# A ninth block of the spectral product moves behind the scans, and sixteen scans move ahead of the attention steps

## The chip, the cores and the metric

The kernel runs on one core of a Trainium2 chip. Its time is the device time of one execution in microseconds (us). The engines are PE (matrix products, with its weight loads listed as PEld), DVE (vector), ACT (activations), POOL (general) and SP, which here only issues DMAs.

## What is computed

Two branches over the same x (2048 x 512) are mixed by a gate; all in float32.

```python
def _A_ref(x, wqkv, wo):
    H = 32; Dh = D // H            # Dh = 16
    q, k, v = ...                  # x @ wqkv, split into heads
    scores = jnp.einsum("bhqd,bhkd->bhqk", q, k) * Dh ** -0.5
    p = _softmax(scores, axis=-1)
    o = jnp.einsum("bhqk,bhkd->bhqd", p, v)
    return o... @ wo

def _B_ref(x, dft_seq_re, dft_seq_im, dft_hid_re, dft_hid_im):
    a = jnp.einsum("bsd,ed->bse", x, dft_hid_re)
    b = jnp.einsum("bsd,ed->bse", x, dft_hid_im)
    return jnp.einsum("ts,bse->bte", dft_seq_re, a) - jnp.einsum("ts,bse->bte", dft_seq_im, b)

g = _sigmoid((x * gate_w).sum(-1, keepdims=True))
return g * _A_ref(x, A_wqkv, A_wo) + (1 - g) * _B_ref(x, ...)
```

## The kernel before

The 32 heads are handled as 16 pairs. For each pair the kernel needs two passes over the scores: a **scan**, which finds the largest score of each query, and a **use**, which computes the scores again, shifted by that maximum, takes the exponential and multiplies with the values. One scan (number n, from 0 to 1023, 64 for each pair) is one block of 128 queries against 512 keys for both heads of the pair: two matmuls and their maxima. Scans run in the order of n all through the kernel.

The order of the work is written out by hand; each engine's queue holds its instructions in the order of the program. It has three stages.

**Projections** (up to about 288 us): q, k, v and the first product of the spectral branch. Products are split into high and low halves, three matmul terms each, and each term is two matmuls in the two 64-row halves of PE (`halves_of`, L184). One such term is called a slot. After each slot `beside` (L262) may issue a scan; the first three pairs (scans 0 to 191) are scanned here as plain scans, one every `PACE` = 3.9 slots.

**Spectral units beside folded scans** (about 288 to 685 us). The second spectral product has 32 blocks of output (16 row blocks for the real and 16 for the imaginary matrix), each four units of 12 slots. The list `coef` holds the units of all but the last `LATER` blocks: with LATER = 8, 96 units, 1152 slots. Beside them run the scans of `FOLDED`. A folded scan (`scan_folded`, L140) uses folded keys: for one head at a time there is one matmul (L153), and then either ACT (L157, for every first of two key blocks) or DVE (L159, for every second, which closes the pair) handles it; the second head's half is issued one scan later (`behind`). So per scan ACT and DVE have one instruction each. A plain scan (`scan_plain`) has two matmuls and, where the narrow banks are used, two DVE reductions. The distance is `FOLD_PACE` slots at the normal pace, and `NARROW` x FOLD_PACE / PACE slots at the start of the stage and where reloaded operands are split (`renew`, from the first half of the last real block to the middle of the first imaginary one). A folded pair has half as many columns of maxima as a plain one (`shift`, L162). With FRONT = 692 the last folded pair, number 10, is cut: 52 of its scans are folded, 12 come as plain scans in the next stage with unfolded rows (`unfolded`), so its maxima tile is first filled with a low number (L150).

**Attention** (685 us to the end): 512 steps, 32 for each pair. A step has the two score products of a key block (`qk2`, four matmuls L209), the exponentials of ACT (L220 for the first, L698 for the second), and the products with the values of the step before (`pv`, L704). Between the two score products stands one further thing: until all scans are done one plain scan (`next_scan`, a double-width one, L134 and L136); from step MIX on, and from both places where `next(fill)` stands, the spectral blocks left over (`spectral`, L824; six matmuls a step, 16 steps a block), and later the output projection. MIX = 1024 - FRONT + 1 is 333, and OUT = MIX + 16 x LATER = 461.

**Rows of queries and keys.** Scans and uses read tiles of the pool `stk`, which has six buffers of one tag. A pair takes two of them, qs and ks. `row_loads` (L88) makes the eight DMAs of a pair (L99), 128 or 256 KB each. In the attention stage all of them are issued by SP, in program order: `load_use(p + 1)` when i == 18, that is at step 32p + 18, and `load_scan` (from `next_scan`) at the scan numbered 54 in its pair. A buffer is handed on when every instruction that touches the tile in it has been issued and done. The row loads of scans in the stage before go through ACT's queue (`load_scan_beside`, at scan 36 of a pair), except `unfolded` and `load_use(0)`, which SP issues two blocks ahead of the end of `coef`.

## Time and profile before

| | us |
|---|---|
| median of 3 runs | 1746.42 |
| lowest and highest | 1744.98, 1747.07 |
| the profiled execution's own time | 1744.77 |
| its span, first to last instruction | 1743.0 |

| stage of the profiled execution | PE busy | DVE busy | ACT busy |
|---|---|---|---|
| 290 to 685 us, units and folded scans | 389.26 | 358.26 | 325.25 |
| 700 to 1320 us, attention with scans | 619.10 | 419.45 | 619.17 |
| 1326 to 1600 us, attention with spectral blocks | 274.00 | 56.00 | 244.14 |

A row of the table of groups reads: line, engine, operation, out<-in, shapes and count; then the time in which at least one of the group ran, the mean time of one in ns, and the idle time of the engine ahead of them with what ended it. A row of waits reads: who waited, for whom, us in total, times, longest. A row of the table of stretches reads: from and to, length, then for each engine the busy time and the count of instructions, and last the granted clock of PE, the busy share of the DMA engines and GB/s. A row of the timeline reads: start, time taken, engine, line, operation, tiles and count. SPq is SP's queue: such a row is the issue of a DMA, not its transfer.

### The profile page before, as it was taken

How to read it: one execution, taken by the hardware profiler on the slowest of the kernel's cores; microseconds unless marked ns; L12 is line 12 of the kernel's file. 1: busy time of each engine (PE TensorE's matmuls, PEld its weight loads, DVE VectorE, ACT ScalarE, POOL GpSimd, SP SyncE). 2: the span in 40 equal slices, each digit the busy share in tenths (PEclk: the TensorE clock that was granted, in tenths of full speed). 3: DMA queues.
4: the chain of work that ended last, by engine and by line, in shares of the span. 5: the costliest groups of instructions: out<-in, count | busy, mean ns of one | idle time of the engine just before them, and what ended most of it. 6: DMA issues, size and time to landing. Idle time of an engine off the chain costs nothing.

```text
span 1743.0 us, 35509 instructions
## 1 busy us (share of the span) xinstructions
PE 1717.7 (99%) x13640; PEld 1026.0 (59%) x13640; DVE 1157.8 (66%) x1876; ACT 1451.7 (83%) x2383; POOL 718.6 (41%) x818
## 2 busy tenths in 40 slices
PE   8999999999999999999999999999999999999998
PEld 7987777888888887333333333333334555555554
DVE  6899998999999887666666666666664212122333
ACT  5445336888888887999999999999999888888885
POOL 3688668555556664032323223232332322322222
PEclk9999999999999999999999999999999999999999
DMA  7782767433344445432332413515313254254712
GB/s 265 256 290 74 223 196 225 120 113 123 99 155 146 143 137 118 71 65 57 61 64 56 92 33 71 87 25 97 77 36 74 68 114 92 67 140 126 190 37 100
DMA packets 126777, 199.54 MB, mean 114 GB/s; under 512 B 53984, under 2 KB 56528, under 8 KB 119696
## 3 DMA queue, kind: packets, MB, share of 16 engines
q1 hardware_dynamic: 84336, 161.02, 34.6%
q0 software_dynamic: 38496, 19.47, 5.3%
q10 hardware_dynamic: 3776, 16.78, 3.6%
q8 instruction: 107, 1.75, 0.4%
q14 instruction: 62, 0.51, 0.1%
HBM read 135.14 MB, written 62.66 MB: 113 GB/s over the span
## 4 chain that ended last, share of the span: by engine, by line
PE 82%; DVE 8%; DMA 4%; POOL 2%; issue 2%; ACT 1%; SPq 0%; DVEq 0%; POOLq 0%; ACTq 0%
PE pvb L704 28%; PE s L209 18%; PE xy L184 17%; PE s L184 8%; PE s L153 7%; DVE mx L136 6%; PE s L134 5%; DMA fa<-ks_d 1%; DMA abr<-ab_d 1%; DMA lc<-ob 1%; DVE fold L159 1%; POOL ab L546 1%; DMA kf_d<-fa 1%; POOL s L252 0%; DMA raws<-wqkv 0%
## 5 line engine op out<-in xcount | busy, mean ns | idle before, releaser
L136 DVE TENSOR_REDUCE mx<-s 128x2 f32<-128x1024 f32 x524 | 627.2, 1223 | 206.4 <-PE s L134 206.4
L220 ACT ACTIVATE eb<-s 128x1024 f32<-128x1024 f32 x513 | 580.2, 1131 | 56.0 <-PE s L209 55.8
L698 ACT ACTIVATE e<-s 128x512 f32<-128x512 f32 x1022 | 609.1, 708 | 1.1 <-PE s L209 1.1
L704 PE MATMUL pvb<-eb,va 128*17 128x512 f32 x2052 | 516.7, 598 | 0.0
L704 PE MATMUL pvb<-e,va 128*17 128x512 f32 x2044 | 515.9, 598 | 0.0
L209 PEld LDWEIGHTS s<-qs,ks 50*128 50x128 f32 x2048 | 211.7, 185 | 368.3 <-ACT eb L220 280.0
L209 PE MATMUL s<-qs,ks 50*128 50x512 f32 x2048 | 427.4, 437 | 0.0
L184 PE MATMUL xy<-b,c 64*128 64x512 f32 x2640 | 418.6, 392 | 1.1 <-ACT c L318 1.1
L159 DVE CUSTOM_DVE_ANT_0 fold<-s,fold 128x512 f32<-128x512 f32 x500 | 338.3, 690 | 36.0 <-PE s L153 17.9
L157 ACT ACTIVATE fold<-s 128x512 f32<-128x512 f32 x500 | 295.7, 602 | 69.7 <-PE s L153 43.3
L184 PEld LDWEIGHTS xy<-b,c 64*128 64x128 f32 x2640 | 294.7, 187 | 19.8 <-ACT c L318 1.4
L153 PE MATMUL s<-ks,qs 48*128 48x512 f32 x1000 | 230.9, 403 | 5.7 <-DVE mx L159 5.2
L134 PE MATMUL s<-ks,qs 48*128 48x512 f32 x1048 | 212.8, 397 | 5.5 <-DVE mx L136 4.9
L716 POOL DMA_DIRECT2D lc<-ob x124 | 62.8, 514 | 298.6 <-DVE ob L713 298.5
L704 PEld LDWEIGHTS pvb<-eb,va 128*17 128x17 f32 x2052 | 69.1, 96 | 190.7 <-issue 182.1
L153 PEld LDWEIGHTS s<-ks,qs 48*128 48x128 f32 x1000 | 125.3, 184 | 44.6 <-DVE mx L159 17.4
L723 POOL DMA_DIRECT2D r_d<-lc x31 | 18.1, 583 | 294.3 <-DVE lc L722 283.0
L350 POOL TENSOR_TENSOR c<-craw,c 128x512 fp32r<-128x512 f32 x92 | 120.3, 1308 | 7.4
L349 POOL CAST c<-craw 128x512 fp32r<-128x512 f32 x92 | 56.7, 617 | 138.4 <-PE xy L184 135.6
L134 PEld LDWEIGHTS s<-ks,qs 48*128 48x128 f32 x1048 | 100.8, 184 | 18.9 <-DVE mx L136 9.9
L184 PE MATMUL xy<-w,b 64*128 64x512 f32 x768 | 106.1, 393 | 1.8 <-ACT ty L451 1.4
L725 POOL DMA_DIRECT2D rb<-r_d x124 | 60.0, 491 | 70.4 <-DMA r_d<-lc 70.4
(128 smaller groups left out, 1508.0 us busy)
## 6 DMA issues: line engine op xcount, KB each, us to landing
craw<-ci SPq DMA_DIRECT2D x64, 256.0 KB
craw<-cr SPq DMA_DIRECT2D x60, 256.0 KB
ks<-k_d SPq DMA_DIRECT2D x46, 256.0 KB
qs<-q_d SPq DMA_DIRECT2D x46, 256.0 KB
ab_d<-ab SPq DMA_DIRECT2D x32, 256.0 KB
y_d<-y SPq DMA_DIRECT2D x32, 256.0 KB
o_d<-oh POOLq DMA_DIRECT2D x28, 256.0 KB, 9.8
o_d<-ol POOLq DMA_DIRECT2D x28, 256.0 KB, 11.4
```

Of the source, the lines that this page charges most:

```text
L134: nc.tensor.matmul(ps[:, j, :], qs[b:b + 48, qb * P:(qb + 1) * P], ks[b:b + 48, c * 512:(c + 1) * 512], start=True, stop=True)
L136: nc.vector.tensor_reduce(mx[p][:, :, qb, c], ps, axis=AX.X, op=ALU.max)
L153: nc.tensor.matmul(ps, qs[b:b + 48, qb * P:(qb + 1) * P], ks[b:b + 48, c * 512:(c + 1) * 512], start=True, stop=True)
L157: nc.scalar.activation(fold[j], ps, AF.Relu)
L159: nc.vector.tensor_tensor_reduce(out=fold[j], in0=ps, in1=fold[j], scale=1.0, scalar=-3.0e38, op0=ALU.add, op1=ALU.max, accum_out=mx[p][:, ...
L184: nc.tensor.matmul(ps[j], lhs[r], rhs[r], start=first, stop=last)
L209: nc.tensor.matmul(pss[j], ks[b:b + 50, kb * P:(kb + 1) * P], qs[b:b + 50, q0:q0 + 512], start=True, stop=True)
L220: nc.scalar.activation(e, ps, AF.Exp, scale=SCALE)
L350: sub(lo, raw, hi.bitcast(F32))
L698: nc.scalar.activation(e[j], pss[j], AF.Exp, scale=SCALE)
L704: nc.tensor.matmul(pvb[r:r + VC, :], va[:, kb, 2 * p + j, :], es[c][j], start=kb == 0, stop=kb == NB - 1, tile_position=(0, r))
L716: nc.gpsimd.dma_start(lc[32 * n:32 * n + 32, :], ob[r + DH:r + VC, :].rearrange("p (s e) -> p s e", e=16))
```

## The change

LATER goes from 8 to 9, so that FRONT goes from 692 to 708: 92 units (1104 slots) and 516 scans stand in the second stage, where 96 units (1152 slots) and 500 scans stood. MIX goes from 333 to 317; OUT stays 461. FOLDED now ends with the last whole pair, at scan 704; the four scans 704 to 707, the first of the pair with the number 11 (the twelfth), are plain ones in the narrow banks. `unfolded` therefore holds pair 11, and is put in the place of the rows when scan 704 is reached. The memset of the maxima goes. FOLD_PACE is 2.05 for 2.19 and NARROW 4.8 for 5.3. SCANS_IN swaps the two wide PSUM banks, since one block fewer uses them in turn.

```diff
-LATER = 8
+LATER = 9
 FRONT = 564 + 16 * LATER
 PACE = 3.9
-FOLDED = range(3 * SCANS, FRONT)
-FOLD_PACE = 2.19
-NARROW = 5.3
+FOLDED = range(3 * SCANS, FRONT // SCANS * SCANS)
+FOLD_PACE = 2.05
+NARROW = 4.8
...
-SCANS_IN = 0
+SCANS_IN = 1
...
                 new_maxima(p)
-                if p == FRONT // SCANS:
-                    nc.gpsimd.memset(mx[p], -3.0e38)
...
-                pace[1] += (PACE / FOLD_PACE if seen[0] in FOLDED else 1.0) / pace[0]
+                pace[1] += (PACE / FOLD_PACE if seen[0] >= FOLDED.start else 1.0) / pace[0]
...
-                    if n % SCANS == 36 and n - n % SCANS + SCANS < FRONT:
+                    if n % SCANS == 36 and n - n % SCANS + SCANS < FOLDED.stop:
                         load_scan_beside(n // SCANS + 1)
...
-                    if seen[0] == FRONT:
+                    if seen[0] == FOLDED.stop:
                         done = behind(n)
+                        scanned.update(unfolded)
...
                 p, i = n // SCANS, n % SCANS
+                if i == 0:
+                    new_maxima(p)
                 qs, ks = scanned[p]
```

## The prediction

> **What bounds the kernel now.** I read the page first, then a table of stages, then who waits for whom in two of them, then SyncE's (SP's) list of transfers, since the change moves work across a point at which buffers change hands.

> ```profile
> span 1743.0 us, 35509 instructions
> PE 1717.7 (99%) x13640; PEld 1026.0 (59%) x13640; DVE 1157.8 (66%) x1876; ACT 1451.7 (83%) x2383; POOL 718.6 (41%) x818
> ```

> PE at 99% is no answer yet: the stages differ. This table has one row for the folded scans beside the spectral units, one for the attention steps with a scan, one for those with a spectral block (PE, PEld, DVE, ACT, POOL busy, clock, DMA):

> ```profile
> 290.00:685.00 395.00, 389.26 (x3253) 336.58 (x3251) 358.26 (x1040) 325.25 (x566) 227.96 (x225) 1.00 0.46 131
> 700.00:1320.00 620.00, 619.10 (x4574) 231.72 (x4566) 419.45 (x389) 619.17 (x981) 182.19 (x275) 1.00 0.33 62
> 1326.00:1600.00 274.00, 274.00 (x2257) 144.85 (x2257) 56.00 (x97) 244.14 (x377) 73.89 (x110) 1.00 0.43 102
> ```

> The front part is PE's, with DVE at 358/395 = 91%. The scan steps are ACT's: 619 of 620 us. The spectral steps are PE's, ACT has 11% to spare. The waits of the scan steps, then two of the front, say the same:

> ```profile
> PEld s L209 <- ACT eb L220: 276.4, 325, 0.9
> ```

> ```profile
> PEld s L153 <- DVE mx L159: 17.4, 48, 2.0
> PE s L153 <- DVE mx L159: 5.2, 10, 1.6
> ```

> In a scan step PE waits 276.4/325 = 0.85 us for ACT's exponential. Nowhere in that stretch does PE wait for a DMA.

> **Sixteen steps change their kind.** Each step has four score matmuls (L209), so a count of them dates a step:

> ```profile
> 700.00:1320.00 620.00, 295.31 (x1306) 137.59 (x1306) 1.00 0.33 62
> 1326.00:1600.00 274.00, 86.72 (x503) 51.33 (x501) 1.00 0.43 102
> ```

> 620/(1306/4) = 1.90 us for a step with a scan, 274/(503/4) = 2.18 us for one with six spectral matmuls. The ninth block turns steps 317 to 332 from the first kind into the second: 16 x 0.28 = **+4.5 us**. Bounds: 4 to 5, both rows being long.

> **The front gets shorter.** It loses 4 units of 24 matmuls and gains 16 scans of two. Where PE is full:

> ```profile
> 310.00:320.00 10.00, 10.00 (x88) 8.80 (x88) 9.12 (x29) 7.98 (x14) 5.25 (x6) 1.00 0.23 82
> ```

> 88 matmuls in 10 us are 0.114 us each, two row halves running at once; other full stretches give up to 0.116, which I take. (96 - 32) x 0.116 = -7.4 us if PE stays the limit. Against it stands DVE:

> ```profile
> L136 DVE TENSOR_REDUCE mx<-s 128x2 f32<-128x1024 f32 x524 | 627.2, 1223 | 206.4 <-PE s L134 206.4
> L159 DVE CUSTOM_DVE_ANT_0 fold<-s,fold 128x512 f32<-128x512 f32 x500 | 338.3, 690 | 36.0 <-PE s L153 17.9 <-ACT fold L157 5.9 <-POOL mx L150 1.3
> L159 DVE DVE_READ_ACCUMULATOR2_ANT mx<- 128x1 f32 x500 | 41.3, 83 | 0.0
> ```

> A folded scan costs DVE (338.3 + 41.3)/500 = 0.76 us in these rows, the second of the two partly under the next fold. Twelve more make 9.1 us; the four plain ones are eight half-width reductions, which no row has, at least 4 x 1.22 = 4.9 us. DVE then has 358.3 + 14 = 372 us in 395 - 7.4 = 388: 96%. At 2.05 slots a scan comes every (2.05 + 1) x 2 x 0.116 = 0.71 us against 0.74 before; in the stretch where DVE also splits reloaded operands the distance falls from 2.98 to 2.52 slots (5.3 x 2.19/3.9, 4.8 x 2.05/3.9). The waits for DVE above, 22.6 us by their sum (they overlap), of which PE's idle is at most 5.7, will grow; I let them take half of the gain: **-3.5 us**. Bounds: -7.4 with no new wait, and +14 if DVE keeps its 36.7 us of idle and becomes the limit (372 + 37 - 395). The poorer end needs DVE idle and limiting at once, so I stay near the other. ACT gets 12 x 0.6 us more where it is busy 82%, and POOL loses four units' splits; neither ends the front. The memset that goes was one instruction off PE's path.

> **A load comes a step too late to find a buffer.** Here lies most of the time. The pool of query and key rows has six tiles, so three pairs. In the attention part two streams draw from it: the rows of the heads in use (asked for at step 18 of every 32, held until that pair's 32 steps are over) and the rows that are scanned (asked for at the scan 54 of 64, held until scan 63). With FRONT = 692 scan 758 is at step 758 - 692 + 1 = 67; with 708 it is at step 51. SP asks in that order, and the trace shows how it goes out:

> ```profile
> SPq L99 <- PE s L209: 257.8, 15, 45.1
> ```

> ```profile
> 750.66 0.56 SPq L99 DMA_DIRECT2D ks<-k_d  x1
> ...
> 811.36 0.56 SPq L99 DMA_DIRECT2D ks<-k_d  x1
> ...
> 815.51 0.42 SPq L99 DMA_DIRECT2D qs<-q_d  x1
> ...
> 933.02 0.56 SPq L99 DMA_DIRECT2D ks<-k_d  x1
> ```

> ```profile
> 684.00:750.66 66.66, 29.41 (x128) 13.04 (x128) 0.97 0.33 61
> 684.00:811.36 127.36, 58.35 (x256) 27.40 (x256) 0.99 0.30 57
> 684.00:933.02 249.02, 116.37 (x512) 53.64 (x512) 0.99 0.32 60
> ```

> Up to these three issues PE had made 128, 256 and 512 score matmuls: exactly 32, 64 and 128 steps. So SP stands at the next load and issues it the moment a pair of heads is done: at 750.66 the rows of pair 2 go into pair 0's place, at 811.36 (step 63 over) the scan rows of pair 12 into pair 1's. Pair 12 was first needed at step 77, thirteen steps later: the load was hidden.

> After the change, at step 51: pair 11's scan rows are held until scan 767 at step 60, pair 1's until step 63, and pair 2's were asked for at step 50 and took pair 0's place. No tile is free. The first to come free is that of pair 11, with scan 767 at step 60; scan 768, the first of pair 12, stands in step 61. So the load can't start before its predecessor's last scan and is wanted one step later. Behind it on SP wait the maxima's store of pair 11 and the loads of step 82, none of them pressing; behind scan 768 on PE waits everything, the step's second score matmuls first, and then ACT. Step 115 (pair 13), 179 and 243 repeat it, since 64 steps are two periods of 32: four waits, for pairs 12 to 15. The front has no such meeting: at its last row loads pair 9 and the reloaded operands have been released.

> The size of one wait: how long the eight transfers of one pair take shows in the DMA column behind the issue at 811.36.

> ```profile
> 811.00:812.00 1.00, 1.00 (x12) 0.14 (x8) 0.89 (x1) 1.00 (x3) 0.00 (x0) 1.00 0.21 66
> 814.00:815.00 1.00, 1.00 (x10) 0.53 (x6) 0.92 (x2) 1.00 (x4) 0.00 (x0) 1.00 1.22 279
> 820.00:821.00 1.00, 1.00 (x11) 0.62 (x14) 0.32 (x2) 1.00 (x3) 0.00 (x0) 1.00 1.23 161
> 824.00:825.00 1.00, 1.00 (x10) 0.38 (x12) 0.51 (x1) 1.00 (x2) 0.00 (x0) 1.00 0.06 9
> 825.00:826.00 1.00, 1.00 (x12) 0.41 (x6) 0.71 (x1) 1.00 (x3) 0.00 (x0) 1.00 0.00 0
> ```

> The last of it falls between 824 and 825: 13.3 us from issue. In the ordinary step the scan and its successor lie as follows:

> ```profile
> 902.09 0.40 PE L134 MATMUL s<-ks,qs 48*128 48x512 f32 x2
> 902.32 0.41 PE L209 MATMUL s<-qs,ks 50*128 50x512 f32 x2
> 903.21 1.19 ACT L698 ACTIVATE e<-s 128x512 f32<-128x512 f32 x2
> 903.99 0.39 PE L134 MATMUL s<-ks,qs 48*128 48x512 f32 x2
> ```

> One scan ends at 902.49, the next begins at 903.99: 1.5 us are covered. The score matmuls behind a scan end at 902.73 and ACT takes them at 903.21, another 0.5. That leaves 13.3 - 1.5 - 0.5 = 11.3 us. PE then starts cold, as it does after the short gap at the head of the attention part (busy PE first, clock in the third column from the right):

> ```profile
> 690.00:692.00 2.00, 1.58 (x14) 0.41 (x12) 0.75 (x1) 1.53 (x3) 0.26 (x1) 1.00 0.00 0
> 692.00:694.00 2.00, 0.91 (x8) 0.32 (x6) 1.23 (x1) 1.57 (x3) 1.92 (x2) 1.00 0.00 0
> 696.00:698.00 2.00, 2.00 (x11) 0.57 (x12) 1.15 (x1) 1.51 (x3) 0.00 (x0) 0.50 1.04 238
> ```

> ```profile
> 695.59 0.79 PE L209 MATMUL s<-qs,ks 50*128 50x512 f32 x2
> 698.60 0.51 PE L209 MATMUL s<-qs,ks 50*128 50x512 f32 x2
> ```

> At clock 0.50 a step took 3.0 us, 1.1 more than 1.90. One such step per wait makes 12.4 us, and four waits **+49.6 us**. Bounds: 4 x 5.7 = 23 if the transfers run at their best rate (second rival), 4 x 13.5 = 54 if two steps run cold.

> [...]

> **Sum.** -3.5 + 4.5 + 49.6 = +50.6 us. The profiled execution took 1744.77 us around its span of 1743.0; the median of the runs is 1746.42, 1.65 above. On the median's scale: 1797.0 us.

> **The rivals.** First, not slower: the load of pair 12 finds a place at once, because some pair's tiles count as free earlier than I think. It decides at one point, whether SP issues that load before step 60. For it: in the trace no scan ever waits for rows. Against it: the three issues above come only when a pair is done, to the step. Then +1.0 us is left, 1747.4 (1743.5 with the front's full gain). A difference under 0.2%, 3.5 us, can't be told from none, so this is "no change". Chance 0.08.

> Second, the waits come but are short: with SP's queue otherwise empty the eight transfers run at the best rate throughout. That rate stands behind the issue at 750.66:

> ```profile
> 753.00:754.00 1.00, 1.00 (x12) 0.47 (x6) 0.93 (x2) 1.00 (x3) 0.00 (x0) 1.00 1.20 295
> ```

> A pair is 4 x 256 + 4 x 128 KB = 1.57 MB; at 295 GB/s 5.3 us, with 1.3 before the first data 6.6 us, which makes 6.6 - 2.0 + 1.1 = 5.7 us a wait, 23 in all, and 1770. Against it: the load at 811.36 had SP's queue to itself as well and took twice that. Chance 0.12. [...]

> Third, DVE becomes the front's limit and the front grows by 14 us: 4.5 + 14 + 49.6 = +68, 1814.5. For it: 96% load with fold after fold. Against: PE's idle of 5.7 us at 91%. Chance 0.08.

> **How the numbers follow.** The forecast has 0.70, the rivals 0.08, 0.12 and 0.08, and 0.02 is for what I don't see. The forecast's own range is 1780 to 1810: waits of 9.5 to 13.5 us each, the front between -7.4 and +2. To hold eight of ten I go down to the second rival, 1770, and up to 1813. Slower by over 0.2% in all but the first rival and a part of the rest: 0.89; within 0.2%: 0.08; faster: 0.03.

> **What would show it.** In the profile after: SP's issue of pair 12's first row load right at the end of a scan matmul, with 240 or so score matmuls before it where there were 256; four gaps of PE and ACT of 10 to 13 us, 64 steps (122 us) apart, PE waiting at L134 for a DMA into ks or qs; clock 0.5 behind each; the front (first unit to first score matmul) 2 to 5 us shorter; steps of 1.90 and 2.18 us otherwise unchanged, the change of kind 16 steps earlier. No gap at step 61 makes the prediction wrong, whatever the rest does; gaps of under 6 us each make the second rival right.

## The result and the profile after

The changed kernel took 1815.7 us (median of 5 runs, 1812.8 to 1816.9) against 1746.25 us before: a ratio of 1.0395, 95% interval 1.0384 to 1.0407. The forecast was 1797.0, with a range of 1770 to 1813. The profiled execution took 1815.1 us, its span is 1813.3 us, 70.3 us above that of before. Its page:

```profile
span 1813.3 us, 35535 instructions
PE 1733.2 (96%) x13640; PEld 1026.4 (57%) x13640; DVE 1153.3 (64%) x1902; ACT 1458.3 (80%) x2393; POOL 708.2 (39%) x807
PE 79%; DVE 7%; DMA 7%; issue 2%; POOL 1%; SPq 1%; ACT 1%; ACTq 0%; DVEq 0%; POOLq 0%
```

PE's share fell from 99 to 96%, and DMA has 7% of the chain that ended last (4% before). The lines of the kernel after are two lower in the functions concerned: score matmuls L207 (209 before), folded scans L151 (153), plain scans L134 as before.

Where the 70.3 us lie shows in stretches cut at the same instructions in both kernels. First the front, from the first folded scan to the first score matmul (PE, PEld, DVE, ACT, POOL busy, clock, DMA), before and then after:

```profile
288.50:684.80 396.30, 390.56 (x3263) 337.73 (x3261) 358.60 (x1041) 326.65 (x569) 229.01 (x226) 1.00 0.46 131
```

```profile
287.40:689.10 401.70, 390.31 (x3201) 332.89 (x3197) 366.77 (x1074) 330.95 (x579) 218.86 (x215) 1.00 0.46 126
```

It is 5.4 us longer, with 62 fewer matmuls on record. PE's idle time in it went from 5.7 us to 11.4, and its busy time stayed at 390 us though 64 matmuls, 7.4 us of work, are gone: more than half of what was lost counts as busy. Next steps 12 to 316, 305 steps with a scan in both kernels, by their score matmuls (1220 = 4 x 305):

```profile
713.66:1292.37 578.71, 276.21 (x1220) 129.02 (x1220) 1.00 0.34 63
1292.37:1323.63 31.26, 14.49 (x64) 6.60 (x64) 1.00 0.12 31
```

```profile
716.38:1358.29 641.91, 280.42 (x1220) 129.00 (x1220) 0.95 0.30 55
1358.29:1393.45 35.16, 11.36 (x64) 6.82 (x64) 1.00 0.22 55
```

They are 63.2 us longer. The second row of each pair is steps 317 to 332, which changed their kind: 3.9 us longer. With -1.6 in the first twelve steps, -1.1 in the projections and +0.5 behind step 332, as the same bounds give them, that is the whole.

Of the 63.2 us, 61.8 lie in four waits: the five steps around each (60 to 64, 124 to 128, 188 to 192, 252 to 256, dated by their first score matmul in both traces) are longer by 15.9, 15.2, 14.9 and 15.8 us. Step 306 has 1.1 more: there DVE splits the operands of the next spectral block, which the kernel before does 16 steps later, in its second row. So the change of kind alone is 3.9 + 1.1 = some 4.9 us. In the waits PE stands eight times for a row load, for two heads in each:

```profile
PE s L134 <- DMA qs<-q_d: 47.4, 8, 6.9
```

The first of the four, in the timeline of PE, ACT and SP's queue:

```profile
807.79 0.50 PE L207 MATMUL s<-qs,ks 50*128 50x512 f32 x2
808.13 0.39 PE L134 MATMUL s<-ks,qs 48*128 48x512 f32 x2
...
808.56 0.56 SPq L99 DMA_DIRECT2D ks<-k_d  x1
...
809.67 0.50 PE L207 MATMUL s<-qs,ks 50*128 50x512 f32 x2
...
813.39 1.33 SPq L99 DMA_DIRECT2D qs<-q_d  x1
...
817.01 0.76 PE L134 MATMUL s<-ks,qs 48*128 48x512 f32 x1 [6.84 <-DMA qs<-q_d]
...
823.05 0.76 PE L134 MATMUL s<-ks,qs 48*128 48x512 f32 x1 [5.28 <-DMA qs<-q_d]
...
824.28 1.08 ACT L699 ACTIVATE e<-s 128x512 f32<-128x512 f32 x2 [12.82 <-PE s L207]
...
826.01 0.79 PE L207 MATMUL s<-qs,ks 50*128 50x512 f32 x2
...
829.42 0.58 PE L207 MATMUL s<-qs,ks 50*128 50x512 f32 x2
```

The scan matmul at 808.13 is scan 767; 0.04 us after its end SP issues the rows of pair 12, and the next scan has to wait for them, its first head until 817.01 and its second until 823.05. ACT stands idle for 12.82 us. Up to that issue PE had made 244 score matmuls, 61 steps' worth, and not 256:

```profile
684.00:808.56 124.56, 54.72 (x244) 25.71 (x244) 1.00 0.24 45
```

The other three begin with issues at 945.88, 1082.39 and 1219.17; the second head's scan matmul starts at 959.75, 1095.74 and 1234.39.

### The profile page after: what moved, and what is told of

Read it like the earlier page. It is cut to its first block, busy times and chain, and to the rows that moved or that the text cites. A ratio compares the mean times of both kernels' runs of the same rounds, so it can differ in the third digit from the quotient of the medians.

```text
span 1813.3 us, 35535 instructions
## 1 busy us (share of the span) xinstructions
PE 1733.2 (96%) x13640; PEld 1026.4 (57%) x13640; DVE 1153.3 (64%) x1902; ACT 1458.3 (80%) x2393; POOL 708.2 (39%) x807
## 4 chain that ended last, share of the span: by engine, by line
PE 79%; DVE 7%; DMA 7%; issue 2%; POOL 1%; SPq 1%; ACT 1%; ACTq 0%; DVEq 0%; POOLq 0%
PE pvb L705 26%; PE s L207 17%; PE xy L182 16%; PE s L182 8%; PE s L151 7%; DVE mx L136 5%; PE s L134 5%; DMA qs<-q_d 3%; DMA lc<-ob 1%; SPq L99 1%; DMA fa<-ks_d 1%; DMA abr<-ab_d 1%; DMA kf_d<-fa 1%; POOL ab L547 0%; DVE fold L157 0%
## 5 line engine op out<-in xcount | busy, mean ns | idle before, releaser
L136 DVE TENSOR_REDUCE mx<-s 128x2 f32<-128x1024 f32 x508 | 607.4, 1222 | 256.7 <-PE s L134 202.6
L699 ACT ACTIVATE e<-s 128x512 f32<-128x512 f32 x1022 | 600.0, 691 | 51.4 <-PE s L207 51.4
L218 ACT ACTIVATE eb<-s 128x1024 f32<-128x1024 f32 x513 | 572.0, 1115 | 73.0 <-PE s L207 73.0
L207 PE MATMUL s<-qs,ks 50*128 50x512 f32 x2048 | 427.9, 439 | 0.0
L207 PEld LDWEIGHTS s<-qs,ks 50*128 50x128 f32 x2048 | 211.9, 186 | 367.4 <-ACT eb L218 259.6
L157 DVE CUSTOM_DVE_ANT_0 fold<-s,fold 128x512 f32<-128x512 f32 x512 | 342.5, 690 | 33.3 <-ACT fold L155 9.8
L155 ACT ACTIVATE fold<-s 128x512 f32<-128x512 f32 x512 | 300.8, 602 | 63.9 <-PE s L151 42.4
L134 PE MATMUL s<-ks,qs 48*128 48x512 f32 x1016 | 209.6, 400 | 54.0 <-DMA qs<-q_d 47.4
L151 PE MATMUL s<-ks,qs 48*128 48x512 f32 x1024 | 250.5, 408 | 11.2 <-DVE mx L157 5.6
L151 PEld LDWEIGHTS s<-ks,qs 48*128 48x128 f32 x1024 | 137.4, 184 | 57.8 <-DVE mx L157 19.4
L134 PEld LDWEIGHTS s<-ks,qs 48*128 48x128 f32 x1016 | 98.1, 186 | 71.2 <-issue 43.9
L351 POOL TENSOR_TENSOR c<-craw,c 128x512 fp32r<-128x512 f32 x88 | 115.5, 1313 | 7.0
L182 PE MATMUL s<-b,chi 64*128 64x512 f32 x606 | 95.4, 390 | 0.3 <-ACT chi L1016 0.3
```

The costliest lines, as they stand in the source:

```text
L134: nc.tensor.matmul(ps[:, j, :], qs[b:b + 48, qb * P:(qb + 1) * P], ks[b:b + 48, c * 512:(c + 1) * 512], start=True, stop=True)
L136: nc.vector.tensor_reduce(mx[p][:, :, qb, c], ps, axis=AX.X, op=ALU.max)
L151: nc.tensor.matmul(ps, qs[b:b + 48, qb * P:(qb + 1) * P], ks[b:b + 48, c * 512:(c + 1) * 512], start=True, stop=True)
L155: nc.scalar.activation(fold[j], ps, AF.Relu)
L157: nc.vector.tensor_tensor_reduce(out=fold[j], in0=ps, in1=fold[j], scale=1.0, scalar=-3.0e38, op0=ALU.add, op1=ALU.max, accum_out=mx[p][:, ...
L182: nc.tensor.matmul(ps[j], lhs[r], rhs[r], start=first, stop=last)
```

## The experiments

Two questions: are the waits a matter of buffers, and why did the front grow?

### The same waits in the kernel before

```diff
-                if i == 18:
+                if i == 1:
                     load_use(p + 1)
```

> The kernel before, with one thing changed: the rows of the next pair in use are asked for at step 1 of every 32 in place of 18. Theory (no free pair of buffers): at steps 3, 67, 131, 195 and 259 the scan rows are then the fourth pair wanted, so five scans wait for rows (pairs 11 to 15), each for about the 15.8 us that a wait takes after the change: 1746 + 79 = 1825 us, with PE waiting at L134 for a DMA. Rival (the waits belong to the denser front, the plain scans or the shifted maxima): nothing of those is here, so 1746 us.

1824.98 us (2 runs; 1746.42 before; ratio 1.0454, interval 1.0433 to 1.0475). The rows of the waits in the attention part:

```profile
PE s L134 <- DMA qs<-q_d: 59.0, 10, 7.1
PEld s L134 <- issue: 57.1, 9, 7.4
PEld s L134 <- DMA ks<-k_d: 5.7, 1, 5.7
```

PE waits ten times for a row load, two heads in each of five waits, and (1824.98 - 1746.42)/5 = 15.7 us is the price of one. Nothing of the change is in this kernel but the order in which two streams ask for one of three pairs of buffers. That order alone makes such waits.

### A fourth pair of buffers

The rows go into a pool of two more tiles, in memory of tiles that are first used at step 292 or later.

```diff
-            cw = pa.enter_context(tc.tile_pool(name="cw2", bufs=2, reuse_waits="tile"))
             ap = pa.enter_context(tc.tile_pool(name="ap", bufs=1, reuse_waits="tile"))
+            cw, ap2 = Opened(), Opened()
+            rows = ExitStack()
+            fourth.append(rows.enter_context(tc.tile_pool(name="stk2", bufs=2)))
...
-                scanned[p], loads = row_loads(p, nc.sync)
+                scanned[p], loads = row_loads(p, nc.sync, pool=stk if p % 2 else fourth[0])
...
+                if step == MIX - 25:
+                    rows.close()
+                    cw.pool = ...    # and ap2, which holds craw and take
```

> The changed kernel with a fourth pair of row buffers for the scan rows of the even pairs, in memory that nothing else uses before step 292. Theory (no free pair): all four waits go, 1815.7 - 4 x 15.8 = 1752.5 us, what is left over the kernel before being the longer front and the 16 steps of the other kind. Rival (the rows are late because SP or the DMA queues are behind, whatever the buffers): the waits stay, 1815 us.

1756.43 us (4 runs; ratio 1.0059, interval 1.0042 to 1.0076), 59.3 below the changed kernel. Steps 12 to 316, by their score matmuls:

```profile
722.10:1301.40 579.30, 275.73 (x1222) 133.52 (x1222) 1.00 0.33 61
```

579.3 us against 578.7 in the kernel before (two matmuls of the next step fall within the rounded bounds): all four waits are gone, and no row of PE waiting for a row load is left in the table of waits of this stretch. The 4 us that are missing from the forecast lie ahead of step 12, which starts 5.7 us later than in the profile of the changed kernel: 3.0 of them in the projections, 1.1 in the front and 1.6 in the first twelve steps. What lengthened these was not tried.

### Scan rows ahead of the rows in use

```diff
-                if n % SCANS == SCANS - 10:
+                if n % SCANS == SCANS - 13:
                     load_scan(n // SCANS + 1)
```

> The changed kernel, with the scan rows asked for three scans sooner (scan 51 of 64, step 48), ahead of the rows in use (step 50). Theory (no free pair): the scan rows get the pair freed at step 31 and come in time, and now the rows in use wait for scan 767 at step 60 and are wanted at step 64, 7.3 us behind it: 17 us for their fourteen loads less 7.3, and 2.9 of cold clock, is some 12.6 us four times over, 1815.7 - 4 x 3.2 = 1803 us, with PE waiting at the score matmuls L207 and not at L134. Rival (the load of the scan rows is only asked for too late): all waits go, 1752 us.

1804.79 us (2 runs; ratio 1.0338, interval 1.0317 to 1.0359). The wait changed its place:

```profile
PE s L207 <- DMA qs<-m_d: 37.0, 5, 9.9
```

The scan rows now come in time, and the score matmuls at the head of a pair wait for the last loads of theirs, the maxima. Asking sooner did not remove the waits while four pairs are wanted and three fit; it picked which load is late.

### Matmuls of no use in the wait

```diff
+                ps = pair_banks()
+                if n % SCANS == 0:
+                    for _ in range(54):
+                        nc.tensor.matmul(ps[:, 0, :], ah[0][0:64, 0:P], ah[0][0:64, :], start=True, stop=True)
-                scan(n, pair_banks())
+                scan(n, ps)
```

> The changed kernel with 54 matmuls of no use (11.6 us at 0.215) ahead of the first scan of each pair of heads in the attention part, into the bank that this scan overwrites. They fill the wait and end before the rows land. Theory (the 2.9 us lost behind each wait, two slow steps, are the array at half clock): the clock stays at 1.0 and 4 x 2.9 = 11.6 us come back, 1804 us. Rival (they are the emptied pipeline between PE and ACT filling again): 1815 us.

1810.7 us (4 runs; ratio 1.0371, interval 1.0356 to 1.0387), between the two. In its profile all that comes before the attention part took 5.7 us more than in that of the changed kernel (first score matmul at 694.8, against 689.1), so that the medians don't decide; the profile does, by the stretch of steps 12 to 316:

```profile
722.10:1354.10 632.00, 276.18 (x1222) 129.22 (x1222) 1.00 0.30 56
```

632.0 us against 641.9: 9.9 of the expected 11.6 came back. By steps, the four waits now cost 12.3, 16.1, 12.3 and 12.7 us. In the changed kernel (first of the fences) the clock, third column from the right, falls within the wait and is still down while the work goes on; with the matmuls (the others) the first wait keeps it:

```profile
813.00:817.00 4.00, 0.00 (x0) 0.02 (x1) 0.00 (x0) 0.00 (x0) 0.00 (x0) 0.50 0.98 151
...
825.00:829.00 4.00, 4.00 (x22) 0.98 (x14) 1.50 (x4) 2.36 (x4) 0.00 (x0) 0.50 0.00 0
829.00:833.00 4.00, 4.00 (x32) 1.37 (x28) 2.17 (x3) 2.96 (x5) 0.00 (x0) 0.92 0.07 12
```

```profile
826.00:830.00 4.00, 4.00 (x26) 2.18 (x25) 1.38 (x3) 1.35 (x3) 0.00 (x0) 1.00 0.18 65
...
964.00:968.00 4.00, 4.00 (x23) 1.11 (x22) 2.44 (x3) 2.65 (x5) 0.00 (x0) 0.57 0.00 0
```

```profile
948.93 12.41 PE L939 MATMUL s<-b 64*128 64x512 f32 x54
961.19 0.40 PE L134 MATMUL s<-ks,qs 48*128 48x512 f32 x1
963.45 0.47 PE L134 MATMUL s<-ks,qs 48*128 48x512 f32 x1 [1.87 <-DMA qs<-q_d]
```

The second row and the timeline's belong to its second wait: there the rows of the second head came 1.87 us after PE had run out of other work, and the clock fell all the same. That is the wait of 16.1 us; in the other three the clock stayed up (1.00 over the whole 632.0 us in the row above, where a second fall of the same 3.4 us would have made it 0.99), and the step behind the first of them took 1.87 us (829.19 to 831.06), where it takes 3.41 in the changed kernel. So the slow steps behind a wait are the half clock and not the pipeline filling. The sum is less clean than the clock: the 54 matmuls took 12.4 us (0.23 each) and not the 11.6 planned, for which 0.215 was my estimate, and in two of the waits the scan starts right behind the last of them, so that there they set the length of the wait together with the rows.

### The reloads one block sooner

```diff
-                    if (ph, t, u) == (0, NB - 3, 0):
+                    if (ph, t, u) == (0, NB - 4, 0):
                         for i in range(2):
                             raw = stk.tile([P, 4, D], F32, tag="stk", name="early")
```

> The changed kernel with the fourth pair of buffers, and with the eight loads of reloaded operands (early) issued one block sooner, at slot 576 in place of 624, so that they stand ahead of the row loads of pair 8 again as in the kernel before (scan 470 against 484; after the change it was scan 494). Theory A (ACT's queue stands behind those loads while it issues its row loads, so that folds, rows and then the clock are late): the gaps of PE at 520 and 533 us and the half clock behind them go, 2.2 + 1.7 + 1.7 us and what DVE and ACT need to catch up, some 7 us: 1756.4 - 7 = 1749.5. Theory B (the front is longer only because DVE is full at the denser pace): 1756.

1752.66 us (6 runs; ratio 1.0031, interval 1.0019 to 1.0044). The reason stands in the timeline of the changed kernel:

```profile
512.56 0.31 ACTq L99 DMA_DIRECT2D qs<-q_d  x1
...
514.79 4.40 SPq L632 DMA_DIRECT2D early<-ab_d  x8
...
518.21 0.58 ACTq L99 DMA_DIRECT2D ks<-kf_d  x1
518.90 1.78 ACT L155 ACTIVATE fold<-s 128x512 f32<-128x512 f32 x3 [2.65 <-DMA early<-ab_d]
...
519.55 0.49 PE L151 MATMUL s<-ks,qs 48*128 48x512 f32 x2 [2.03 <-ACT fold L155]
...
531.31 0.47 PE L151 MATMUL s<-ks,qs 48*128 48x512 f32 x1 [1.86 <-DMA qs<-q_d]
```

SP puts eight loads of 256 KB between two of pair 8's row loads, which ACT's queue issues. ACT doesn't issue its next one until the first of those has landed (at 518.19, the issue follows at 518.21), and its folds stand behind it; then the rows themselves are late. What holds ACT is a semaphore of the program, a counter that an instruction waits for, and not a full queue: in the trace all loads of SP and ACT share eight semaphores (100, 101, 104, 105 and 107 to 110), the issue at 518.21 waits for 101, and 101 is the one that the first of SP's eight loads raises. The issue at 520.09 waits for 104, that of the second. With the reload sooner these gaps are gone:

```profile
289.90:687.70 397.80, 389.78 (x3199) 332.40 (x3197) 366.60 (x1074) 331.21 (x579) 218.84 (x215) 1.00 0.46 127
```

397.8 us for the stage, and 402.8 in the run with the fourth pair alone: 5.0 of the 7 expected, 3.8 in the medians. (This run, the next and the one with half of the columns have the fourth pair too.)

### Splits moved from DVE to POOL

```diff
-                        after(4, (nc.gpsimd if s % 4 == 3 else nc.vector).tensor_sub, al[s], raw, ah[s].bitcast(F32))
+                        after(4, (nc.gpsimd if s % 2 else nc.vector).tensor_sub, al[s], raw, ah[s].bitcast(F32))
```

> As the run with the sooner reload, and every second in place of every fourth of the reloaded operands is split on POOL and not on DVE. Theory B for the stretch of the reloads (DVE is full there; gaps of 3.8 us between 570 and 587): 3 to 4 us less, 1746. Rival (POOL, which needs 1.3 us for a split and also prepares the coefficients, becomes late in its place): the same or slower than the run with the sooner reload, 1749 to 1755.

1748.04 us (11 runs; ratio 1.0017, interval 1.0006 to 1.0027), with a front of

```profile
290.40:684.70 394.30, 386.54 (x3201) 331.89 (x3197) 363.85 (x1070) 331.17 (x579) 223.51 (x219) 1.00 0.47 128
```

3.5 us less, as the theory of the full DVE has it; the rival, a POOL that becomes late, did not come true. Only 0.3 us of it are idle time of PE (8.0 to 7.8); the rest is busy time of the same matmuls.

### The denser pace alone, and with the reload sooner

```diff
-FOLD_PACE = 2.19
-NARROW = 5.3
+FOLD_PACE = 2.05
+NARROW = 4.8
```

> The kernel before with only the two paces of the change (2.05 and 4.8): the same slots and scans, the scans merely end some 80 slots sooner. Theory A and B together: what the pace did to the front after the change shows here alone, 7 us by the meeting of the loads (the reload comes at scan 494 here too) and 4 by DVE: 1746.4 + 11 = 1757. Rival (the pace is free, and the front is long for the shorter row of slots or the four plain scans): 1746.

> The kernel before with the two paces of the change and the reload one block sooner. Theory A: the 7 us of the meeting go, 1750, and what is left over 1746 is DVE's share. Theory B alone: as the run with the paces only.

1766.53 us (4 runs; ratio 1.0114, interval 1.0093 to 1.0134) and 1759.95 us (4 runs; 1.0079, 1.0066 to 1.0093). The difference of the two, 6.6 us, is the meeting of the loads, as expected. The level is not: 20 us over the kernel before where 11 were expected. One part is an effect of the experiment: the scans end early, the rest of the slots pass faster, and the first score matmul waits for the rows that SP loads for it, here 4.5 us and 5.2 in the second run.

```profile
PE s L209 <- DMA qs<-m_d: 4.5, 1, 4.5
```

So these two runs show that the pace is not free and that the meeting costs some 6 us (6.6 in the medians, 413.1 - 407.2 = 5.9 in the stage); they don't size DVE's share, and some 8 to 9 us of the 20 stay open.

### Half of the columns in DVE's folds

```diff
-                nc.vector.tensor_tensor_reduce(out=fold[j], in0=ps, in1=fold[j], ...
+                nc.vector.tensor_tensor_reduce(out=fold[j][:, 0:256], in0=ps[:, 0:256], in1=fold[j][:, 0:256], ...
```

> As the run with every second split on POOL (1748.0), but DVE's fold works on 256 of its 512 columns, so half of the keys of every second block is left out of the maxima of pairs 3 to 10. Same instructions, about half of DVE's time in the front. Theory B (what is left of the front's loss is DVE at 94% making PE late in small pieces): the stage comes from 394.3 to near the 389 us that its matmuls alone need, 1743 us. Rival (it is ACT at 86%, or the rows): 1748.

1741.42 us (11 runs; ratio 0.9983, interval 0.9974 to 0.9992). The stage:

```profile
288.70:679.30 390.60, 384.44 (x3199) 317.98 (x3197) 243.47 (x1070) 324.41 (x579) 222.95 (x219) 0.99 0.47 129
```

With DVE at 243/391 = 62% in place of 364/394 = 92% the same matmuls take 3.7 us less, while ACT's time hardly changes (324 for 331): of the 5.4 us that were left over 396.3 - 7.4 = 388.9, 3.7 were DVE's. (The medians differ by 6.6 and the two profiled executions by 5.4, of which 1.7 lie ahead of this stage.) This kernel leaves half of the keys of every second block out of the maxima; it is a measurement and no version to keep.

### The splits moved in the kernel before

The same line as above, in the kernel before.

> The kernel before with every second in place of every fourth of the reloaded operands split on POOL. Theory B (DVE is the tight engine where operands are reloaded, at the old pace too: PE idles 1.1 us of the 60 between 540 and 600): 1 to 2 us less, 1744.5. Rival (DVE has room there at the old pace): 1745.6, no change.

1744.93 us (11 runs; ratio 0.9998, interval 0.9989 to 1.0007): no change that can be told. The stage is 395.2 us in the profile, 1.1 less than the 396.3 before, so that an effect of 1 us, the lower end of what was expected, is not excluded. No version that does the whole computation was faster than the kernel before.

## Why the prediction was right and where it was wrong

**The four waits** were right in place, cause and number: the issue right behind scan 767, PE waiting at L134 for the rows, 137 us apart (64 steps and one wait), for pairs 12 to 15. The run with the fourth pair removes them, and the run with the rows in use asked for earlier makes five of them in the kernel before. The first rival falls.

**The size of one wait** was the term that was too small: 12.4 us forecast, 61.8/4 = 15.5 measured. Three pieces of it. From issue to the second head's matmul the rows took 14.5 us in the first wait (808.56 to 823.05) and 13.9, 13.4 and 15.2 in the others, 14.2 in the mean, where I had 13.3 from the traffic behind one issue. I took off 0.5 us for score matmuls that wait for ACT in the ordinary step; behind the wait PE at half clock is the late one (ACT takes the scores at 824.28, 0.04 us after their end), so nothing was to be taken off. And I let one step run slow, at +1.1: the rest of step 61 (823.05 to 826.01) and all of step 62 (826.01 to 829.42) ran at half clock, 2.9 us more than they take otherwise. 14.5 - 1.5 + 2.9 = 15.9 is what was measured in the first wait; over the four the slow steps cost 2.7 in the mean, which makes 14.2 - 1.5 + 2.7 = 15.4. So the slow steps are half of what was missed. The upper bound of 13.5 had the second slow step, but not the longer load, and kept the 0.5. The transfers themselves were not slower than forecast: by the packets of SP's queue in the trace the last bytes of the eight loads end 13.7, 12.9, 12.5 and 14.1 us behind the issue, and 13.7 behind the issue at 811.36 in the kernel before. What I left out is the 0.8 to 1.1 us from the last packet to the matmul that waits for it. The second rival, a load at the best rate in 6.6 us, is further off still: the rate of 295 GB/s that it takes from one microsecond was not kept up behind any of these issues: in the third microsecond behind them SP's packets moved 270 to 295 GB/s, in the fifth 33 to 123.

**The front** failed by its sign: -3.5 us forecast, +5.4 measured (-7.4 in matmuls, so 12.8 lost). The step that failed is "The front has no such meeting". I looked there at the buffers only, which do suffice, and not at the order of the issues: at the denser pace slot 624, where the reload is asked for, falls on scan 494 and no longer on scan 474, so the reload stands in the middle of pair 8's row loads, which begin at scan 484. That costs 5.0 and 5.9 us of the stage by the two pairs of runs with and without the sooner reload. The other step, that DVE takes half of the gain, was low: moving splits off DVE gave 3.5 us and halving its folds another 3.7. The three runs together take the stage from 402.8 to 390.6. The reason given for staying near the better end, PE's idle time of 5.7 us, did not bound anything: more than half of the loss counts as busy time of PE. A stretch of 3.41 us at half clock, from 532.67 in the changed kernel, can make up 1.7 us of that, an estimate: half of it; how the rest comes about was not looked into. The third rival named the right engine for that half, with a bound of +14 that was too high.

**The sixteen steps** came out at some +4.9 for +4.5, the split in step 306 counted. The parts of the sum thus missed by 61.8 - 49.6 = 12.2 us in the waits and 8.9 in the front; the small ones together give back about 1.4.

## What to carry to other kernels

When work is moved by some steps, redraw who holds each buffer at each step: two streams that share a pool are free of waits only by their phase, and a shift of 16 steps that costs some 5 us in arithmetic cost 62 in waits. Do the same for the issues of loads and the semaphores that they share: a pace counted in one unit moves every issue that is counted in another, and what used to stand ahead of a group of loads may land in the middle of it. For a wait on a critical engine, add the time from the last byte to the first instruction that needs it, here 0.8 to 1.1 us, and the slow time after it, here 2.7 of 15.5 us, a sixth of the whole. And an engine's idle time is no bound for what a late neighbour costs it: with splits off DVE the front was 3.5 us shorter, and PE's idle time 0.3.

## What the runs showed of the hardware that was not expected

It fell behind a short gap too. In the second wait with the useless matmuls the gap was 1.87 us, and the records have the fall at 964.46 (0.57 in 964 to 968, in the fence above). In the 3.41 us before that fall PE was busy for 45% of the time; before the four falls in the waits of the changed kernel for 30, 53, 53 and 0%. At the end of a stretch of the same length with 60% (1218.74 to 1222.15) there was no fall: the clock stayed at 1.00 until 1225.57.
